# Block 0 of a fused SSM and GEGLU kernel: gate/up with the contraction outermost over three token tiles and 512 columns, in place of two tiles and 896 columns

## The chip, the cores and the metric

One core of one Trainium2 chip. The metric is the device time of one execution in microseconds; the kernel before is given by the median of five runs.

## The reference

```python
def reference(A_x, A_Lambda_re, ..., B_w_gate, B_w_up, B_w_down):
    def _A_ref(x, Lambda_re, Lambda_im, B_re, B_im, C_re, C_im, log_dt, Dskip):
        ...
        Bu = jnp.einsum("bld,pd->blp", x + 0j, B_bar)
        for t in range(L):
            h = Lam_bar[None, :] * h + Bu[:, t, :]
            hs.append(h)
        hseq = jnp.stack(hs, 1)
        return 2.0 * jnp.einsum("blp,dp->bld", hseq, Cmat).real + x * Dskip[None, None, :]

    def _B_ref(x, w_gate, w_up, w_down):
        return (_gelu(x @ w_gate) * (x @ w_up)) @ w_down

    x = A_x                        # 1 x 2048 x 512, bf16
    xn = _layernorm(x, axis=-1)
    return x + _A_ref(xn, ...) + _B_ref(xn, B_w_gate, B_w_up, B_w_down)
```

The token count is 2048, the width D is 512, the state size P is 512 and the hidden width F of the gated part is 1376. All inputs and the output are bf16.

## The kernel before

The 2048 tokens are four blocks of 512, and a block is four tiles of 128 tokens. For each block the kernel normalizes the rows (VectorE, with a power on GpSimd), transposes them to XNT by DMA, multiplies by the gate and up weights (`GU`), by the input matrix of the state recurrence (`BU`), scans the states on VectorE (`CHAIN`), and multiplies hidden values and states by the output matrices into one bank per tile (`DN`), which VectorE adds to the skip term and SP stores. PSUM has eight banks of 512 f32 columns.

An operation is declared with what it reads and writes. A list scheduler (`Sched`) orders VectorE, ScalarE and GpSimd by estimated durations and priorities; TensorE and SP issue in the order of the program text. `order_behind` and `ch` fix an order on one engine where the text wants one. SP's queue carries nearly all DMAs, ScalarE's queue the second X tile and three parameter rows.

Block 0 is handled apart, since nothing is there to overlap with at the start. Its gate/up product for the first 896 columns uses rows that are only centred: `cent` and `sub` subtract the mean, `cent_T` transposes a tile on TensorE into PSUM and an engine (ScalarE but for the first piece) copies it to XC, and the scale 1/sqrt(var) of a token is put in later, because a token is a PSUM partition here. `GT_k` is one matmul of one contraction slice k (128 of the 512), tile j and column range u of `FR` (three ranges of 256 columns, one of 128), for gate, up or both side by side; `GT_mm` is a whole unit, all four slices of one tile and range into one bank. `GT_evac` evicts a unit: a GELU with the scale on ScalarE (L718), a product with the scaled up half on VectorE (L724), into H0. Later `H0_T` transposes H0 by DMA.

The text order of block 0 before is this. Two tiles (0 and 1) have all seven 128-column pieces accumulated with k outermost, in seven banks (`acc`: three per tile, one shared for the 128-wide ranges): k = 0 gate then up, k = 1 gate then up, k = 2 and k = 3 both at once. `GT_evac` follows each range as k = 3 ends. Tiles 2 and 3 then run as units, each behind the eviction of the bank it takes. The weights come in slices of 896 columns per k (`ld_wk`, 224 KB each, gate and up in turn on SP), and one load each for columns 896 to 1376 (`ld_w`). The X tiles 2 and 3 are loaded ahead of and behind the last pair of slices.

The statistics of tiles 0 and 1 give a first `root` (L613, L614, L619), whose scales `rss` the evictions need; tiles 2 and 3 have their own. `norms` (L626) writes the normalized rows of a tile, and `TR` (L737) transposes them by DMA into XNT. The four of block 0 go through SP in turn, and `GU(0, [7, 8, 9, 10])` (L844), the columns from 896 on, follows block 0's units on TensorE and reads all of XNT of block 0. From there on TensorE's order is `GU`, `BU`, `DN` of the blocks, and this text is the same in both kernels.

Of the kernel before, what the change touches and what calls it, by code (L numbers as in the profile page):

```python
# [9 lines left out]
ALU = mybir.AluOpType  # L10
# [351 lines left out]
def build(nc, ins, out):  # L362
    with ExitStack() as es:
# [15 lines left out]
        WD = A.alloc("WD", [KF, D], BF16)  # L379
        FS = 896  # L380
        WGc = [Buf("WGc%d" % i, "sbx", 10 * i, 10 * i + 1) for i in range(KD + 1)]
        WUc = [Buf("WUc%d" % i, "sbx", 100 + 10 * i, 101 + 10 * i) for i in range(KD + 1)]
        wdeps = lambda Wc, ft: Wc[0:KD] if 128 * ft < FS else [Wc[KD]]
        WDc = [Buf("WDc%d" % i, "sbx", 200 + 10 * i, 201 + 10 * i) for i in range(2)]
# [96 lines left out]

        def ld_wk(W, Wc, src, k, queue="sync", after=()):
            return S.dma(lambda e: e.dma_start(W.ap[:, k, 0:FS], src[128 * k:128 * (k + 1), 0:FS]),
                         256 * FS, writes=[Wc[k]], tag="ld_w", queue=queue, after=after)

        def ld_w(W, Wc, src):
            return S.dma(lambda e: e.dma_start(W.ap[:, :, FS:F], src[:, FS:F].rearrange("(k p) f -> p k f", p=128)),
                         1024 * (F - FS), writes=[Wc[KD]], tag="ld_w")

        def ld_x0(j, queue="sync", after=()):  # L490
            return S.dma(lambda e, j=j: e.dma_start(X[j].ap, x2[128 * j:128 * (j + 1), :]), 128 * 1024, writes=[X[j]], tag="ld_x0", queue=queue, after=after)
        ld_x0(0)
        GATE["par"] = S.order_behind(ld_x0(1, "scalar", [wrm]), GATE["table"])
        for k in range(KD):
            if k == 3:
                ld_x0(2)
            ld_wk(WG, WGc, ins["B_w_gate"], k)
            ld_wk(WU, WUc, ins["B_w_up"], k)
        ld_x0(3)

# [20 lines left out]
        def load_W():  # L521
            ld_w(WG, WGc, ins["B_w_gate"])
            ld_w(WU, WUc, ins["B_w_up"])

# [164 lines left out]
        def acc(j, u):  # L689
            return (3, 256 * j) if u == 3 else (4 * j + u, 0)  # L690

        def GT_k(k, j, u, ws, first=False):
            f0, f1 = FR[u]
            w = f1 - f0
            bank, c0 = acc(j, u)
            dst = PS[bank][:, c0 + w * ws[0]:c0 + w * (ws[-1] + 1)].rearrange("p (w f) -> p w f", w=len(ws))
            PE(lambda e: e.matmul(dst, XCd(j, k), WGU[:, ws[0]:ws[-1] + 1, k, f0:f1], start=first, stop=k == KD - 1, skip_group_check=True),  # L697
               d_pe([w * len(ws)]), [(WGc, WUc)[w_][k] for w_ in ws] + [XCs[j][k > 0]] + ([] if first else [BANK[bank]]), [BANK[bank]], "GK")

        def GT_mm(j, u, bank):  # L700
            f0, f1 = FR[u]
            w = f1 - f0
            dst = PS[bank][:, 0:2 * w].rearrange("p (w f) -> p w f", w=2)

            def f(e):
                ins_ = None
                for k in range(KD):
                    ins_ = e.matmul(dst, XCd(j, k), WGU[:, :, k, f0:f1], start=(k == 0), stop=(k == KD - 1))  # L708
                return ins_
            PE(f, d_pe([2 * w] * KD), WGc[0:KD] + WUc[0:KD] + XCs[j], [BANK[bank]], "GT")  # L710

        def GT_evac(js, r, bank, rss, c0s=(0,)):
            f0, f1 = FR[r]
            w = f1 - f0
            todo, gelus = [], []
            for j, (sc, rb), c0 in zip(js, rss, c0s):
                GATE["nh"] = kk = (GATE["nh"] + 1) % 3
                gelus.append(ACT(lambda e, kk=kk, c0=c0, sc=sc: e.activation(GG[kk].ap[:, 0:w], PS[bank][:, c0:c0 + w], ACTF.Gelu_apprx_tanh, scale=sc),  # L718
                                 d_act(w, 1), [BANK[bank], rb], [GG[kk]], "gelu"))
                todo.append((j, sc, rb, c0, kk))  # L720
            GATE["last_gelu"] = gelus[-1]
            for j, sc, rb, c0, kk in todo:
                hp = Buf("H0_%d_%d" % (j, r), "sb", H0[j].lo + 2 * f0, H0[j].lo + 2 * f1)
                V(lambda e, j=j, kk=kk, c0=c0, sc=sc: e.scalar_tensor_tensor(H0[j].ap[:, f0:f1], PS[bank][:, c0 + w:c0 + 2 * w], sc, GG[kk].ap[:, 0:w],  # L724
                                                                             ALU.mult, ALU.mult),
                  d_dve_1x(w), [BANK[bank], GG[kk], rb], [hp], "hmul", after=gelus)

# [79 lines left out]
        def GU_rest(b):  # L807
            k2, ft = b % 2, KF - 1
            f0, m = 128 * ft, FROWS[ft]
            for i in range(2):  # L810
                bank = next_bank()

                def f(e, i=i, bank=bank):
# [6 lines left out]
                    return ins_  # L820
                PE(f, d_pe([2 * m] * 8), [WGc[KD], WUc[KD]] + XTr(b), [BANK[bank]], "GR%d" % b)
                GATE["nh"] = kk = (GATE["nh"] + 1) % 3
# [149 lines left out]
        fill(4)  # L972
        GT_k(0, 0, 0, [0], True)
        cent_T(1, 0, 1, 6)
        for u in (1, 2, 3):
            GT_k(0, 0, u, [0], True)
        cent_T(0, 1, 4, 7)
        cent_T(1, 1, 4, 5)
        for u in range(4):
            GT_k(0, 0, u, [1])  # L980
        for us in ((0, 3, 2), (1,)):
            for w_ in range(2):
                for u in us:
                    GT_k(0, 1, u, [w_], w_ == 0 and u < 3)
        ch(*stats(0, 0)); ch(*stats(0, 1))
        op, mn0, qb0, rq0 = root(0, 0, 2)
        ch(op)
        ch(recip(qb0, rq0))
        for j in range(2):
            ch(norms(0, [j], mn0, rq0, 0))  # L990
        TR(0, [0, 1])
        ch(*stats(0, 2)); ch(sub(2))
        ch(*stats(0, 3)); ch(sub(3))
        op, mn2, qb2, rq2 = root(0, 2, 4)
        ch(op)
        ch(recip(qb2, rq2))
        rss = [(rq.ap[:, i:i + 1], rq) for rq in (rq0, rq2) for i in range(2)]
        for w_ in range(2):
            for j in range(2):
                for u in range(4):  # L1000
                    GT_k(1, j, u, [w_])
        for j in range(2):
            for u in range(4):
                GT_k(2, j, u, [0, 1])
        for j, u in ((0, 0), (0, 1), (0, 2), (1, 0), (1, 1), (1, 2), (0, 3), (1, 3)):
            if (j, u) == (1, 0):
                cent_T(2, 0, 4, 7)
            GT_k(3, j, u, [0, 1])
            if u < 3:
                GT_evac([j], u, acc(j, u)[0], rss[j:j + 1])  # L1010
        GT_evac((0, 1), 3, 3, rss[0:2], (0, 256))
        def unit(j, u, bank):
            GT_mm(j, u, bank)
            GT_evac([j], u, bank, rss[j:j + 1])
        unit(2, 0, 0)
        unit(2, 1, 1)
        cent_T(3, 0, 4, 7, c0=512)
        for (j, u), bank in zip([(2, 2), (2, 3), (3, 0), (3, 1), (3, 2), (3, 3)], (2, 4, 5, 6, 3, 7)):
            unit(j, u, bank)
        rstate["n"] = 0  # L1020
        norms(0, [2, 3], mn2, rq2, 2)
        TR(0, [2, 3])
# [90 lines left out]
```

## Time and profile before

| What | Value |
|---|---|
| median of five runs | 178.16 us (177.79, 177.87, 178.16, 179.15, 179.3) |
| profiled execution's own time | 178.16 us |
| its span | 176.8 us, 2527 instructions |
| TensorE busy | 173.7 us, 98% |
| VectorE busy | 159.2 us, 90% |
| ScalarE busy | 95.2 us, 54% |
| first matmul of block 0's gate/up | 4.56 us |
| first L844 matmul | 18.94 us |

The span runs from the first to the last instruction of the program; the own time is longer by what lies around it. "PE" is TensorE, "PEld" its weight loads, "DVE" VectorE, "ACT" ScalarE, "POOL" GpSimd and "SP" the engine that issues DMAs. Matmuls overlap one another in the profile: each is drawn until its modelled end, so the distance between the starts of two matmuls, not the length of one, is what a matmul takes of TensorE's time. A line of the timeline or of the chain has the start, the length and the instruction, with the idle time before it and its releaser in brackets.

### The profile page before, as it was taken

The page shows a single profiled execution, that of the slowest core. Times are in us where ns is not written, and L with a number is a line of the kernel's source. Part 1 is how long each engine was busy: PE and PEld are TensorE (multiplying, and loading weights), DVE is VectorE, ACT ScalarE, POOL GpSimd, SP SyncE. Part 2 cuts the span into 40 slices and gives each one's busy share as a digit, 9 for nine tenths or more (in the row PEclk, how much of TensorE's full clock was granted, in tenths as well). Part 3 has the DMA queues.
Part 4 walks back from the last instruction along what each step waited for, and adds up shares of the span by engine and source line. Part 5 has one row for each costly group of instructions (what it writes and reads, how often), then busy time and mean ns, then how long its engine had stood idle before and what let it go on. Part 6 is the DMA issues. An engine that isn't in the chain of part 4 may idle for free.

```text
span 176.8 us, 2527 instructions
## 1 busy us (share of the span) xinstructions
PE 173.7 (98%) x895; PEld 85.3 (48%) x895; DVE 159.2 (90%) x279; ACT 95.2 (54%) x185; POOL 10.3 (6%) x24
## 2 busy tenths in 40 slices
PE   8999999999999999999999999999999999999995
PEld 3845464644644444444644444444464444444453
DVE  5779799995989999879999999989999999999931
ACT  4258576999976899257676594000657880000000
POOL 3222040200300000000200000000000000000000
PEclk9999999999999999999999999999999999999999
DMA  5994799178599500001134000002001000000311
GB/s 176 360 280 63 200 193 206 33 140 155 112 227 333 97 0 2 0 30 59 33 61 89 0 0 0 4 0 89 30 0 33 0 0 0 0 0 0 122 67 54
DMA packets 31364, 14.36 MB, mean 81 GB/s; under 512 B 23704, under 2 KB 31352, under 8 KB 31352
## 3 DMA queue, kind: packets, MB, share of 16 engines
q1 hardware_dynamic: 31184, 14.07, 33.4%
q8 instruction: 7, 0.11, 0.3%
q10 hardware_dynamic: 168, 0.13, 0.2%
q14 instruction: 5, 0.04, 0.1%
HBM read 6.46 MB, written 2.10 MB: 48 GB/s over the span
## 4 chain that ended last, share of the span: by engine, by line
PE 95%; DMA 2%; DVE 1%; ACT 1%; issue 0%; DVEq 0%
PE PS L885 37%; PE PS L844 32%; PE PS L750 16%; PE PS L697 3%; PE PS L818 3%; DMA arena<-arena 2%; PE PS L934 2%; DVE arena L724 1%; PE PS L676 1%; PE PS L708 1%; ACT arena L718 0%; PE PS L941 0%; ACT arena L683 0%; DVE arena L626 0%; DVE arena L903 0%
## 5 line engine op out<-in xcount | busy, mean ns | idle before, releaser
L885 PE MATMUL PS<-arena 128*128 128x512 bf16 (+3 forms) x323 | 66.2, 367 | 0.0
L844 PE MATMUL PS<-arena 128*128 128x512 bf16 x264 | 58.1, 380 | 0.3 <-DMA arena<-arena 0.3
L885 PEld LDWEIGHTS PS<-arena 128*128 128x128 bf16 (+1 forms) x323 | 30.8, 98 | 35.2
L844 PEld LDWEIGHTS PS<-arena 128*128 128x128 bf16 x264 | 25.7, 98 | 30.8 <-issue 0.5
L788 DVE TENSOR_TENSOR_SCAN arena<-arena 128x512 bf16<-128x512 f32 x32 | 38.7, 1254 | 0.0
L859 ACT ACTIVATE arena<-PS 128x512 bf16<-128x512 f32 x33 | 19.8, 600 | 25.6 <-DVE arena L903 16.1
L750 PE MATMUL PS<-arena 128*128 128x512 bf16 (+1 forms) x136 | 28.1, 367 | 0.0
L863 ACT ACTIVATE arena<-PS 128x512 bf16<-128x512 f32 x33 | 19.8, 600 | 5.5 <-PE PS L844 5.5
L750 PEld LDWEIGHTS PS<-arena 128*128 128x128 bf16 x136 | 13.3, 98 | 14.1
L877 ACT ACTIVATE PS<-arena 128x512 f32<-128x512 bf16 (+2 forms) x17 | 9.4, 575 | 18.6 <-DVE arena L903 18.1
L759 ACT ACTIVATE arena<-PS 128x512 bf16<-128x512 f32 x32 | 17.8, 592 | 2.0 <-PE PS L750 2.0
L903 DVE TENSOR_TENSOR arena<-PS,arena 128x512 bf16<-128x512 f32 (+2 forms) x17 | 10.9, 653 | 7.3 <-PE PS L885 7.2
L865 DVE TENSOR_TENSOR arena<-arena 128x512 bf16<-128x512 bf16 x33 | 13.2, 418 | 2.1 <-ACT arena L863 2.1
L777 DVE TENSOR_TENSOR arena<-arena 128x4096 bf16<-128x4096 bf16 (+1 forms) x5 | 9.2, 1861 | 0.9 <-ACT arena L603 0.9
L775 DVE TENSOR_TENSOR arena<-arena 128x4096 bf16<-128x4096 bf16 (+1 forms) x5 | 9.2, 1861 | 0.3 <-ACT arena L602 0.3
L800 DVE TENSOR_TENSOR arena<-arena 128x4096 bf16<-128x4096 bf16 x4 | 9.2, 2289 | 0.0
L801 DVE TENSOR_TENSOR arena<-arena 128x4096 bf16<-128x4096 bf16 x4 | 9.2, 2288 | 0.0
L607 DVE BATCH_NORM_STATS2 arena<-arena 128x6 f32<-128x512 bf16 x12 | 7.8, 680 | 1.1 <-DMA arena<-in_A_x_dram 0.9
L718 ACT ACTIVATE arena<-PS,arena 128x256 bf16<-128x256 f32 (+1 forms) x16 | 6.3, 446 | 4.4 <-DVE arena L608 3.7
L724 DVE SCALAR_TENSOR_TENSOR arena<-PS,arena 128x256 bf16<-128x256 f32 (+1 forms) x16 | 6.4, 445 | 1.0 <-PE PS L676 0.7
L697 PE MATMUL PS<-arena 128*128 128x256 bf16 (+2 forms) x48 | 7.2, 301 | 0.0
L708 PE MATMUL PS<-arena 128*128 128x512 bf16 (+1 forms) x32 | 6.5, 353 | 0.0
(96 smaller groups left out, 126.2 us busy)
## 6 DMA issues: line engine op xcount, KB each, us to landing
out_dram<-arena SPq DMA_DIRECT2D x15, 128.0 KB, 1.7
arena<-in_A_x_dram SPq DMA_DIRECT2D x3, 512.0 KB, 5.4
arena<-in_B_w_down_dram SPq DMA_DIRECT2D x1, 1280.0 KB, 7.9
arena<-in_B_w_gate_dram SPq DMA_DIRECT2D x4, 224.0 KB, 4.1
arena<-in_B_w_up_dram SPq DMA_DIRECT2D x4, 224.0 KB, 4.2
arena<-in_B_w_gate_dram SPq DMA_DIRECT2D x1, 480.0 KB, 5.7
arena<-in_B_w_up_dram SPq DMA_DIRECT2D x1, 480.0 KB, 6.5
arena<-arena SPq DMA_TRANSPOSE x25, 3.0
```

Source lines behind the costliest of these rows:

```text
L697: PE(lambda e: e.matmul(dst, XCd(j, k), WGU[:, ws[0]:ws[-1] + 1, k, f0:f1], start=first, stop=k == KD - 1, skip_group_check=True), d_pe([w ...
L750: ins_ = e.matmul(PS[bank][:, 128 * j0:128 * j1], BBT[c][dk].ap[:, 128 * s:128 * (s + 1)], XNT[b].ap[:, dk, 128 * j0:128 * j1], start=(dk ...
L759: GATE["evBu"] = ACT(lambda e, bank=bank, k3=k3, s=s, c=c: e.activation(SSc[k3][s][c].ap, PS[bank][:, :], ACTF.Copy), d_act(512), [BANK[ba ...
L775: V(lambda e, s0=s0, s1=s1: e.tensor_tensor(TA.ap[:, s0:s1], ssb.ap[:, s0:s1], cos4[:, s0:s1], ALU.mult), d_dve_tt2x(1024 * step), [ss, CO ...
L788: V(lambda e, g=g, rb=rb, init=init: e.tensor_tensor_scan(g.ap, rb, g.ap, init, ALU.mult, ALU.add), d_dve_scan(512), [g, PA[RRr]] + ([CARc ...
L844: ins_ = e.matmul(PS[bank][0:m, c0:c1], W.ap[:, dk, 128 * ft:128 * ft + m], XNT[b].ap[:, dk, c0:c1], start=(dk == 0), stop=(dk == KD - 1))
L859: GATE["last_gelu"] = ACT(lambda e, bg=bg, kk=kk, m=m: e.activation(GG[kk].ap[0:m, :], PS[bg][0:m, :], ACTF.Gelu_apprx_tanh), d_act(512), ...
L863: ACT(lambda e, bu=bu, kk=kk, m=m: e.activation(UPB[kk].ap[0:m, :], PS[bu][0:m, :], ACTF.Copy), d_act(512), [BANK[bu]], [UPB[kk]], "evU")
L865: V(lambda e, kk=kk, m=m, ft=ft, k2=k2: e.tensor_tensor(HTt[k2][ft].ap[0:m, :], GG[kk].ap[0:m, :], UPB[kk].ap[0:m, :], ALU.mult), d_dve_tt ...
L877: ACT(lambda e: e.activation(PS[bank][:, c0:c1], X[tt].ap[:, c0:c1], ACTF.Copy), d_act(c1 - c0), [X[tt]], [BANK[bank]], "seed")
L885: ins_ = e.matmul(PS[bank][:, c0:c1], l_[:, 128 * j:128 * (j + 1)], r_[:, c0:c1], start=False, stop=last and n == len(ops) - 1, skip_group ...
L903: V(lambda e: e.tensor_tensor(OUTB[ko].ap[:, c0:c1], PS[bank][:, c0:c1], XD[tt].ap[:, c0:c1], ALU.add), d_dve_1x(c1 - c0), [BANK[bank], XD ...
```

## The change

The contraction-outermost part takes three tiles (0, 1 and 2) and the first 512 columns, two banks for each tile, six in all. Slices of the weights are loaded per k for 512 columns (128 KB), columns 512 to 896 come as one load for gate and one for up, and columns 896 to 1376 as before. The X tile 2 is now loaded ahead of the second pair of slices, tile 3 ahead of the fourth. One `root` serves tiles 0 to 2, another tile 3. What is left, both halves of tile 3 and columns 512 to 896 of all tiles, runs as ten units. `GT_evac` takes one unit at a time. The diff, cut to its core:

```diff
-        FS = 896
-        ...
-        wdeps = lambda Wc, ft: Wc[0:KD] if 128 * ft < FS else [Wc[KD]]
+        FC = [(0, 512), (512, 896), (896, F)]
+        ...
+        wdeps = lambda Wc, ft: Wc[0:KD] if ft < 4 else [Wc[KD + (ft > 6)]]
...
         for k in range(KD):
-            if k == 3:
-                ld_x0(2)
+            if k in (1, 3):
+                ld_x0((k + 3) // 2)
             ld_wk(WG, WGc, ins["B_w_gate"], k)
             ld_wk(WU, WUc, ins["B_w_up"], k)
-        ld_x0(3)
+        ld_w(WG, WGc, ins["B_w_gate"], 1)
+        ld_w(WU, WUc, ins["B_w_up"], 1)
...
         def acc(j, u):
-            return (3, 256 * j) if u == 3 else (4 * j + u, 0)
+            return 2 * j + u
...
-        GT_k(0, 0, 0, [0], True)
+        def ks(k, j, w_, first=False):
+            for u in range(2):
+                GT_k(k, j, u, w_, first)
+        ks(0, 0, [0], True)
         cent_T(1, 0, 1, 6)
-        for u in (1, 2, 3):
-            GT_k(0, 0, u, [0], True)
+        ks(0, 0, [1])
         cent_T(0, 1, 4, 7)
+        ks(0, 1, [0], True)
         cent_T(1, 1, 4, 5)
-        for u in range(4):
-            GT_k(0, 0, u, [1])
-        for us in ((0, 3, 2), (1,)):
-            for w_ in range(2):
-                for u in us:
-                    GT_k(0, 1, u, [w_], w_ == 0 and u < 3)
-        ch(*stats(0, 0)); ch(*stats(0, 1))
-        op, mn0, qb0, rq0 = root(0, 0, 2)
+        ks(0, 1, [1])
+        for j in range(2):
+            ks(1, j, [0, 1])
+        ch(*stats(0, 2)); ch(sub(2)); ch(*stats(0, 0)); ch(*stats(0, 1))
+        op, mn0, qb0, rq0 = root(0, 0, 3)
         ch(op)
+        ch(*stats(0, 3)); ch(sub(3))
         ch(recip(qb0, rq0))
+        op, mn3, qb3, rq3 = root(0, 3, 4)
+        ch(op)
+        rss = [(rq0.ap[:, i:i + 1], rq0) for i in range(3)] + [(rq3.ap, rq3)]
         for j in range(2):
             ch(norms(0, [j], mn0, rq0, 0))
+        ch(recip(qb3, rq3))
         TR(0, [0, 1])
-        ch(*stats(0, 2)); ch(sub(2))
-        ...
-        for w_ in range(2):
-            for j in range(2):
-                for u in range(4):
-                    GT_k(1, j, u, [w_])
+        cent_T(2, 0, 4, 7)
         for j in range(2):
-            for u in range(4):
-                GT_k(2, j, u, [0, 1])
-        for j, u in ((0, 0), (0, 1), (0, 2), (1, 0), (1, 1), (1, 2), (0, 3), (1, 3)):
-            ...
-            GT_k(3, j, u, [0, 1])
-            if u < 3:
-                GT_evac([j], u, acc(j, u)[0], rss[j:j + 1])
-        GT_evac((0, 1), 3, 3, rss[0:2], (0, 256))
-        ...
-        unit(2, 0, 0)
-        unit(2, 1, 1)
-        cent_T(3, 0, 4, 7, c0=512)
-        for (j, u), bank in zip([(2, 2), (2, 3), (3, 0), (3, 1), (3, 2), (3, 3)], (2, 4, 5, 6, 3, 7)):
-            unit(j, u, bank)
-        rstate["n"] = 0
-        norms(0, [2, 3], mn2, rq2, 2)
+            ks(2, j, [0, 1])
+        for k in range(3):
+            ks(k, 2, [0, 1], k == 0)
+        for j in range(3):
+            ks(3, j, [0, 1])
+            for u in range(2):
+                GT_evac(j, u, acc(j, u))
+            if j == 0:
+                cent_T(3, 0, 4, 6)
+        for (j, u), bank in zip([(3, 0), (3, 1), (0, 2), (0, 3), (1, 2), (1, 3), (2, 2), (2, 3), (3, 2), (3, 3)],
+                                (7, 6, 0, 1, 2, 3, 4, 5, 0, 7)):
+            GT_mm(j, u, bank)
+            GT_evac(j, u, bank)
+        rstate["n"] = 2
+        norms(0, [2], mn0, rq0, 0)
+        norms(0, [3], mn3, rq3, 3)
         TR(0, [2, 3])
```

## The prediction, as it was put on record

> **What bounds the kernel now.** I read the busy shares first, then the chain that ended last in order of time, then the waits of TensorE, and last the timelines of the opening, matmul by matmul.
>
> ```profile
> PE 173.7 (98%) x895; PEld 85.3 (48%) x895; DVE 159.2 (90%) x279; ACT 95.2 (54%) x185; POOL 10.3 (6%) x24
> PEclk9999999999999999999999999999999999999999
> ```
>
> TensorE is busy for 98% of a span of 176.8 us. The profiled execution's own time is 178.16 us, which is also the median of the five runs; 1.36 us lie around the span. A busy TensorE is not one at its peak, so I looked for lost time in its start times.
>
> ```profile
> 18.80 0.14 issue
> 18.94 5.34 PE PS L844 x24
> ...
> 129.76 12.09 PE PS L844 x56
> 141.85 32.91 PE PS L885 x171
> 174.75 0.02 issue
> ```
>
> These are pieces of the chain: start, length, what. From 18.94 us to 174.75 us it is TensorE alone. Take 56 matmuls of 512 columns in 12.09 us: 0.216 us each. All pieces behind 18.94 run at this rate with no hole, so whatever the change does must show in when the first L844 (the remaining gate/up columns of block 0 from the transposed tile) starts, or as a new wait behind it.
>
> ```profile
> 0.77 3.14 PE L934 MATMUL PS<-const-bfloat16-1.0 128*128 128x512 bf16 x7 [0.77 <-PEq L1098]
> ...
> 4.56 0.37 PE L697 MATMUL PS<-arena 128*128 128x256 bf16 x1
> 6.01 0.32 PE L697 MATMUL PS<-arena 128*128 128x256 bf16 x1
> ...
> 12.69 0.38 PE L708 MATMUL PS<-arena 128*128 128x512 bf16 x1
> 13.07 0.38 PE L708 MATMUL PS<-arena 128*128 128x512 bf16 x1
> 18.27 0.38 PE L708 MATMUL PS<-arena 128*128 128x256 bf16 x2
> 18.94 0.59 PE L844 MATMUL PS<-arena 128*128 128x512 bf16 x2 [0.29 <-DMA arena<-arena]
> ```
>
> The timeline gives start, length and count. The seven warming matmuls start 0.427 us apart, twice 0.216, so TensorE runs at half rate at first although the granted clock reads full throughout; single starts show the full rate from about 6.1 us. After that there are three holes, by start to start less the matmul's own column time: 7.20 to 7.26 (0.07), 12.91 to 13.07 (0.17, waiting for a bank's eviction), and 18.48 to 18.94 (0.46). The column "idle" shows only 0.29 of the last, because the modelled end of a matmul lies behind its column time. Together 0.69 us: all that an order of work in block 0 can win back at an unchanged clock.
>
> ```profile
> PE PS L844 <- DMA arena<-arena: 0.3, 1, 0.3
> PEld PS L708 <- ACT arena L718: 0.5, 1, 0.5
> 13.62 0.16 DVE L619 RECIPROCAL arena<-arena 128x2 f32<-128x2 bf16 x1
> 14.93 0.40 DVE L626 TENSOR_SCALAR arena<-arena 128x512 bf16<-128x512 bf16 x1
> ```
>
> The last hole waits for the fourth transposing DMA of block 0. Its source, the normalized tile 3, is ready at 15.33 us, and that DMA lands 3.3 us after its issue at 15.49.
>
> **The change, part by part.**
>
> *Column work.* Both orders put 28,672 columns of gate/up and the same 16 transposes through TensorE. 80 matmuls become 68. One of 256 columns starts 0.109 after its forerunner, one of 512 0.216, so twelve fewer save 12 x 0.002 = 0.02 us. Up to 6.1 us both orders are at half rate with work at hand, so the end of block 0 moves only by holes.
>
> *Loads.* SP's thirteen loads ahead of the transposes become fifteen; two more issues at 0.47 us put the transposing queue entries back from 7.04 to 7.98. The first of these has its data from the norm, which I place at 10.3 us, so that is hidden; without this cover it costs 0.9. For landings I use bytes in queue order: before, 480 KB had landed at 4.0 us, 704 at 5.4, 928 at 6.2, 1152 at 6.7, 1376 at 7.2, 1600 at 7.9, 2304 at 9.8. After, first up slice: 512 KB, 4.2 to 4.6 us; X tile 2: 640 KB, 5.0; second pair: 896 KB, 6.1; third: 1152 KB, 6.7; X tile 3: 1280 KB, 7.0; fourth: 1536 KB, 7.7; columns 512 to 896: 2304 KB, 9.8.
>
> *TensorE's new order,* from the unchanged 4.56 us. The first up slice is wanted at 5.08 (two matmuls at 0.21, one transpose at 0.107): there. The first contraction of both tiles ends at 6.56. The second needs tile 0's evicted transposes: their last ends at 6.03, ScalarE takes 0.49, so TensorE goes on at 6.60: a wait of 0.04, where before sixteen matmuls covered this eviction. Tile 1's eviction ends at 6.98, wanted at 7.03. The second pair of weights is wanted at 6.60 (0.5 spare). Transposes of tile 2 at 7.46, third contraction 7.69 to 8.55 (weights 1.0 spare), tile 2's eviction (0.60) ends at 8.48. Tile 2's three contractions end at 9.85, the fourth wants its weights then (2.1 spare). Tile 3's transposes at 10.28, contractions to 11.37, its eviction ends at 11.25. Ten units remain: two of four 512-column matmuls (1.73) to 13.09, then four pairs of a 512 and a 256 unit (0.86 + 0.44) to 18.28.
>
> *VectorE.* Tile 2's statistics now come first: 5.0 + 0.69 + 0.18 + 0.35 is 6.3, wanted at 7.46. Two more statistics (0.87 each), root (0.17 + 0.71 on GpSimd, covered by tile 3's statistics and subtraction, 1.3) and reciprocal give the scales at 9.8; the first GELU wants them at 10.26. Sixteen products at about 0.41 run from 10.8, three normalizations between. Each bank is wanted a unit of 0.43 to 0.86 us later than its product ends: bank 0 at 13.09 against 11.2, bank 4 at 15.69 against 13.8. So the 0.17 hole goes. Tile 3 is normalized at about 13.4 in place of 15.33; its transposing DMA, at 3.3 to 4.1 us, lands at 16.8 to 17.6, before 18.28. So the 0.46 hole goes. One wait is new in VectorE's queue: a parameter product now stands ahead of six products and waits for GpSimd's power, which waits for the parameters' transpose (13.4 before, some 14 now, plus 1.0). It is reached at 15.7. Queued behind it are the products that free bank 2 for L844; these have 1.9 us spare.
>
> *Behind 18.28.* The next X load leaves SP some 2 us earlier, so VectorE's 0.95 us idle at 21.5 shrinks. ScalarE's sine table and VectorE's scans had their results early: 69.9 against a use at 74.4, and 162.0 against 165.4. A shift of 0.7 breaks none.
>
> The sum: 0.69 + 0.02 - 0.04 = 0.67, taken as 0.65 us. 178.16 - 0.65 = **177.5 us**.
>
> A rule of the Trainium skill speaks against the change ("DMA: Bandwidth & Descriptors", section "Bandwidth"): batch transfers to 1 MiB or more, 64 KB reaching 138 GB/s and 1 MB 341, measured there on loads that GpSimd issued. Were 128 KB loads limited to 138 GB/s, 1536 KB would land at about 13.4 us (an estimate, with 2 us fixed), 3.5 us late, and the sum would read 181. The trace has many loads in flight at once, so I do not take it:
>
> ```profile
> 4.56:6.10 1.54, 1.54 (x13) 1.41 (x13) 1.51 (x5) 0.28 (x1) 0.00 (x0) 1.00 0.97 336
> ```
>
> 336 GB/s with 224 KB loads queued; no row has 128 KB loads alone. From below, each can land no sooner than the first X tile, 2.1 us after issue: no wait either, the same sum. From above, each could keep the latency after issue that the 224 KB loads had (3.7 to 4.4 us); that is the first rival.
>
> **The rivals.**
>
> 1. *The loads are no quicker.* The second up slice lands at 3.08 + 4.1 = 7.2, not 6.6: 0.6 lost; the third at 4.02 + 4.4 = 8.4, another 0.1. The gain is used up: **178.2 us**. For it: SP's issue at 0.47 us each paces small loads. Against: the latencies rose with the bytes queued, and those are fewer.
>
> 2. *The wait before L844 stays.* If the last transposing DMA takes the 5.3 us that block 0's first took, it lands at 13.45 + 5.3 = 18.75, and 0.14 us is left of the gain: **178.0 us**. Against: that first one had loads ahead of it until 12.9.
>
> 3. *Slower: the clock.* Should the first up slice land at 1.66 + 3.7 = 5.4, TensorE stands still for 0.3 us at 5.08, longer than any hole it had before 6.1 (0.19, ahead of 4.56). If the full rate needs the 5.3 us of nearly unbroken work seen from 0.77 to 6.1 over again, half rate lasts to 10.7: 4.6 us at half rate cost 2.3. 178.16 - 0.65 + 0.3 + 2.3 = **180.1 us**. It decides from a landing later than about 5.3 us.
>
> On this the Trainium skill ("TensorE: Matmul & The Clock Gate", Part 1: The HAM clock gate) says that a free-running window of about 3.4 us decides, not a length of unbroken work since the start. By it one more window at half rate would cost 1.7 us, 179.5 in place of 180.1, and a run's luck would move the moment of full rate.
>
> That the change does nothing is excluded: the instruction lists show 68 matmuls and the split loads.
>
> **How the numbers follow.** A measurement of this kernel tells about 1% from no change. Forecast 0.56 (own range 177.1 to 177.9); rival 1 0.16, rival 2 0.08, rival 3 0.10; 0.10 for what I have not seen, half on each side. Within 1% (176.4 to 179.9) lie the forecast and rivals 1 and 2: 0.80. Slower 0.10 + 0.05 = 0.15, faster 0.05: a gain of 1.8 us has no place in the holes. The range's low end takes 0.75 us of the half rate between 4.56 and 6.1 away as well: 176.8. Its high end is rival 1 with the 1.1 us by which the runs of before exceeded their median: 179.3. Rival 3 and what is unseen stay outside, 0.2.
>
> **What would show it.** Right: the first L844 near 18.3 us with no DMA wait, tile 3 normalized near 13.4, no hole over 0.1 between 6.1 and 18.3, and everything behind shifted alike. Rival 1: TensorE idle for a DMA of weights at 6.6. Rival 3: 256-column matmuls still 0.21 apart behind 6.5 us. The prediction is wrong if block 0 ends at 18.3 and a hole opens later, at the sine tables (35 to 46 us) above all.

## The result, and the profile after

| What | before | after |
|---|---|---|
| median over all comparisons | 177.91 us (90 runs) | 177.41 us (48 runs) |
| ratio, 95% interval | | 0.9964, 0.9952 to 0.9975 |
| profiled execution's own time, span | 178.16, 176.8 us | 177.23, 175.9 us |
| first L844 (after: L842) | 18.94 us | 18.27 us |

The gain is 0.50 us by the medians, 0.36%. It is shown, and under the 1% that a measurement of a few runs tells from no change. The forecast was a gain of 0.65 us and 177.5 us. The long runs are gone as well: 12 of the 90 runs before took 179.0 us or more (up to 179.56; 4 of 75 in the runs of before that go with the experiments below), while the longest of the 48 after took 178.44. By the means the gain is 0.65 us (178.03 to 177.38).

The page of the kernel after, engines' busy time and counts, and from its last part the loads of weights (count, KB each, median us from issue to landing):

```profile
PE 173.2 (98%) x883; PEld 84.1 (48%) x883; DVE 159.7 (91%) x279; ACT 95.5 (54%) x185; POOL 10.7 (6%) x24
...
arena<-in_B_w_gate_dram SPq DMA_DIRECT2D x4, 128.0 KB, 2.9
arena<-in_B_w_up_dram SPq DMA_DIRECT2D x4, 128.0 KB, 3.2
```

There are twelve matmuls fewer. Before, the slices of 224 KB took 4.1 us (gate) and 4.2 us (up) by the median; the smaller ones land a microsecond sooner after their issue.

Pieces of the chain after (start, length, what):

```profile
6.31 0.22 PE PS L700 x2
6.53 0.05 issue
6.58 1.02 PE PS L700 x4
...
129.09 12.09 PE PS L842 x56
141.18 32.91 PE PS L883 x171
174.08 0.02 issue
```

The 56 matmuls of this L842 piece take the same 12.09 us as before and begin 0.67 us earlier (129.09 against 129.76), as L842 itself does: in this pair TensorE's work behind block 0 is unchanged. The span is 0.9 us shorter; the other 0.2 us lie behind the last matmul (2.06 us to the end of the span against 2.29), and a section below takes them up.

The waits after (engine, line, waited for: us in total, times, longest), and the timelines of TensorE and VectorE (start, length, what, idle time and its releaser in brackets):

```profile
DVE arena L553 <- POOL arena L552: 0.8, 1, 0.8
PE PS L932 <- PEq L1089: 0.8, 1, 0.8
PEld PS L700 <- ACT arena L686: 0.5, 2, 0.3
```

```profile
17.83 0.60 PE L711 MATMUL PS<-arena 128*128 128x256 bf16 x4
18.27 0.59 PE L842 MATMUL PS<-arena 128*128 128x512 bf16 x2
```

```profile
9.31 0.17 DVE L622 RECIPROCAL arena<-arena 128x3 f32<-128x3 bf16 x1
...
12.92 0.40 DVE L629 TENSOR_SCALAR arena<-arena 128x512 bf16<-128x512 bf16 x1
...
16.32 0.16 DVE L553 TENSOR_TENSOR arena<-arena 128x4 f32<-128x4 bf16 x1 [0.78 <-POOL arena L552]
```

L842 starts with no wait for a DMA; before, L844 had one. Tile 3 is normalized at 13.32 us (15.33 before), and its transposing DMA lands at 16.69 us, 1.6 us ahead of its use. One hole is left from 6.1 us on: 0.22 us at 6.58, where the second contraction of tile 0 waits for ScalarE's eviction (L686). VectorE's new wait for GpSimd is there, 0.78 us, and TensorE has no hole behind it ahead of L842.

### The profile page after: what moved, and what is told of

It is laid out like the page before. It is cut to its first block, busy times and chain, and to the rows that moved or that the text cites. A ratio compares the mean times of both kernels' runs of the same rounds, so it can differ in the third digit from the quotient of the medians.

```text
span 175.9 us, 2509 instructions
## 1 busy us (share of the span) xinstructions
PE 173.2 (98%) x883; PEld 84.1 (48%) x883; DVE 159.7 (91%) x279; ACT 95.5 (54%) x185; POOL 10.7 (6%) x24
## 4 chain that ended last, share of the span: by engine, by line
PE 98%; DVE 0%; issue 0%
PE PS L883 37%; PE PS L842 32%; PE PS L748 16%; PE PS L711 4%; PE PS L700 3%; PE PS L816 3%; PE PS L932 2%; PE PS L679 1%; PE PS L939 0%; DVE arena L901 0%
## 5 line engine op out<-in xcount | busy, mean ns | idle before, releaser
L842 PE MATMUL PS<-arena 128*128 128x512 bf16 x264 | 58.1, 380 | 0.0
L842 PEld LDWEIGHTS PS<-arena 128*128 128x128 bf16 x264 | 25.7, 98 | 30.3
L748 PE MATMUL PS<-arena 128*128 128x512 bf16 (+1 forms) x136 | 28.1, 367 | 0.0
L711 PE MATMUL PS<-arena 128*128 128x512 bf16 (+1 forms) x40 | 7.1, 337 | 0.0
L700 PE MATMUL PS<-arena 128*128 128x512 bf16 (+1 forms) x28 | 6.6, 366 | 0.1
```

What stands on the lines that cost most here:

```text
L748: ins_ = e.matmul(PS[bank][:, 128 * j0:128 * j1], BBT[c][dk].ap[:, 128 * s:128 * (s + 1)], XNT[b].ap[:, dk, 128 * j0:128 * j1], start=(dk ...
L842: ins_ = e.matmul(PS[bank][0:m, c0:c1], W.ap[:, dk, 128 * ft:128 * ft + m], XNT[b].ap[:, dk, c0:c1], start=(dk == 0), stop=(dk == KD - 1))
```

## Three executions of each kernel: what belongs to the program

One profiled execution is one draw. Each kernel was profiled twice more, and one further kernel (`e8_sp_shift`, below) has block 0 exactly as before. "Full rate from" is the start of the first matmul of block 0, transposes included, from which starts lie 0.056 us (128 columns), 0.109 us (256) or 0.216 us (512) apart; holes are those behind it. In some profiles the records of 15 matmuls are missing (TensorE x880 in place of x895); each leaves a gap of 0.216 us that is no hole, and where it was the first L844 or L842, its start is put that much ahead of the first one shown.

| execution | full rate from | holes ahead of L844 / L842 | L844 / L842 | 4th transposing DMA landed | last matmul's start to end of span | own time |
|---|---|---|---|---|---|---|
| before | 6.16 | 0.07 + 0.17 + 0.46 | 18.94 | 18.80 | 2.29 | 178.16 |
| before_again | 4.62 | 0.28 + 0.17 | 18.05 | 17.56 | 2.35 | 177.43 |
| before_third | 4.67 | 0.05 + 0.17 | 17.88 | 17.38 | 2.50 | 177.53 |
| e8_sp_shift | 5.36 | 0.07 + 0.17 | 18.19 | 17.68 | 2.12 | 177.20 |
| after | 5.58 | 0.22 | 18.27 | 16.69 | 2.06 | 177.23 |
| after_again | 4.77 | 0.15 + 0.07 | 17.88 | 16.94 | 2.06 | 176.84 |
| after_third | 5.37 | 0.11 + 0.11 + 0.21 | 18.38 | 16.96 | 2.05 | 177.50 |

For after, L842 starts at 17.56 us + half of (full rate from, less 4.6) + holes in all three executions, to 0.02 us (the expectation had put 17.75 in place of 17.56); for before the constant comes out between 17.47 and 17.62. The constants agree, so the column work of block 0 is the same in both kernels. Behind block 0 there are three more holes: 0.08 us at 32.4 in before_again, 0.17 at 24.5 in before_third, 0.14 at 32.8 in after_third.

What was expected of the further executions:

> The kernel before once more, for a second profile of the same program. Theory (the moment of TensorE's full rate moves from execution to execution, 4.6 to 6.2 us in the profiles so far, and costs half of its distance; the rest is holes): with an earlier full rate the holes of before are not smaller than 0.69 us in sum, since the weights and the normalizations do not come earlier with it. Rival: the holes are the same three with the same lengths whatever the clock does.

> The kernel after, unchanged, looked at a second time: which of its readings belong to the program and which to one execution. Theory (the end of block 0 is set by TensorE's column work plus its holes, and the moment of full rate is free): the first L842 starts at 17.75 + half of (moment of full rate - 4.6) + holes, so between 17.8 and 18.8 us for a moment between 4.6 and 6.6; no wait for a transposing DMA ahead of it (landed by 17.3 at the latest); one hole of 0.1 to 0.3 at tile 0's eviction near 6.6 when full rate comes before 6.0, none above 0.1 when it comes later. Rival (full rate comes earlier because of the new order of work): full rate again within 0.2 us of the 5.58 us of the first look.

> The kernel before, unchanged, looked at a third time. Theory (two limits that change places with the moment of full rate): with full rate before 5.2 us a hole of 0.2 to 0.4 at the first up slice and the last transposing DMA of block 0 landed in 2.4 to 2.6 us; with full rate after 6 us no hole there. The wait ahead of L844 goes by the landing of that DMA alone: 3.3 us or more and it is there with 0.3 to 0.5 us, 2.6 us or less and it is gone. Rival (the wait belongs to the program): L844 again waits 0.3 to 0.5 us for the DMA, whatever the moment.

> The kernel after, unchanged, looked at a third time, for the same question as its second look: first L842 between 17.8 and 18.8 us, at 17.75 + half of (moment of full rate - 4.6) + holes; no wait for a transposing DMA. Rival: the moment of full rate again within 0.2 us of 5.58 us.

Two of these were missed: the holes of before_again add up to 0.45 us ahead of L844, not to 0.69 or more, and before_third, with early full rate, had 0.05 us at the first up slice in place of 0.2 to 0.4 (its part on the transposing DMA, 2.5 us and no wait, was met). The two of after were met in the range of L842's start, in the absence of a wait for a transposing DMA, and against their rival (full rate at 4.77 and 5.37 us, not within 0.2 us of 5.58); the constant, and in after_again the holes, came out otherwise.

The 0.46 us wait ahead of L844 is not a constant of the kernel before. This is line L737, its transposing DMAs issued between 13 and 17 us, in the first execution of before, then in the second:

```profile
L737 SPq DMA_TRANSPOSE arena<-arena x2: 1189/1680/2172, 14.3 to 15.5; - x2
...
DMA to landing us min/median/max: 3.3/3.7/4.1
```

```profile
L737 SPq DMA_TRANSPOSE arena<-arena x2: 1191/1228/1264, 13.8 to 15.1; - x2
...
DMA to landing us min/median/max: 2.4/2.5/2.5
```

The same two DMAs need 3.3 and 4.1 us in one execution, 2.4 and 2.5 in the other, and in the second L844 waits for none. The DMA view shows what sets the slow ones apart; the first execution of before, 14 to 19 us (a queue with packets, MB and share; DMAs with median us to landing):

```profile
q8 instruction: 1, 0.02, 1.3%
...
arena<-arena SPq DMA_TRANSPOSE x2, 3.7
```

The first line is one packet of 16 KB on a queue (q8) of kind "instruction", at 16.20 us, while packets of the third transposing DMA were still being moved. Such a packet falls among the packets of a transposing DMA of tile 2 or 3 in three of this study's 14 profiles, and these are the three with a slow one: before (16.20 us, 4.1 us to landing), e1 (14.87, 4.3) and e6 (19.56, 4.0), the latter two described below. In the other eleven it comes when the data of these DMAs has been moved, at 17.11 us at the earliest (e3), and none of them has a delay of this kind. The fourth DMA of before, issued behind the third, landed 0.47 us after it. No run moved this packet alone, so its part is seen in all profiles but not tested; what places it was not found.

The second execution has a hole of its own instead; the waits and TensorE's timeline of before_again:

```profile
PEld PS L697 <- DMA arena<-in_B_w_up_dram: 0.3, 1, 0.3
```

```profile
5.05 0.50 PE L676 MATMUL PS<-arena 128*128 128x128 bf16 x6
5.67 0.28 PE L697 MATMUL PS<-arena 128*128 128x256 bf16 x1
```

Full rate came early, TensorE ran out of work at 5.39 us, and the first up slice landed at 5.62. In before_third it landed at 5.44 and the hole was 0.05: the landing decides there, and not the moment of full rate alone, as the expectation had put it. So the kernel before has two loose ends, the first up slice and tile 3's transposing DMA, each late in some executions. In after the up slice landed at 4.39 to 4.76 us and the DMA 0.9 to 1.6 us ahead of L842 in all three. That margin is what the change has for certain; what it is worth differs from execution to execution. It fits the long runs that only before has, but none of those was profiled, so what made them long is not shown.

## Experiments on block 0

The ratios below are each against runs of before on the same chip, with their 95% interval.

**Is the early normalization enough?** e1 puts the root of tiles 2 and 3, and their normalization, ahead of products in the kernel before, with its loads as they are. e2 only lets the transposes of tile 3 fill the 0.17 us hole. e3 does both. (In e1, e3 and e6 two parameter products on VectorE are also held until the last GELU, so that they don't take the place that is made free.)

```diff
# e1_norm_early, on before; root (and norm of tile 2) as a condition of an early product
+        early[0, 0] = op
...
+                early[1, 0] = norms(0, [2], mn2, rq2, 2)
...
+        norms(0, [3], mn2, rq2, 2)
...
-        norms(0, [2, 3], mn2, rq2, 2)
```

```diff
# e2_fill, on before
         unit(2, 0, 0)
-        unit(2, 1, 1)
         cent_T(3, 0, 4, 7, c0=512)
+        unit(2, 1, 1)
```

> The kernel before, with its loads and its order on TensorE, but with tiles 2 and 3 normalized earlier on VectorE (root ahead of the first product, tile 2's normalization ahead of the fourth). Theory (the gain of the change is holes on TensorE, the largest the wait of the first L844 for the fourth transposing DMA): that DMA is issued near 14.9 us in place of 15.49 and lands near 18.3, the hole of 0.46 us shrinks to below 0.1, the hole of 0.17 at 12.9 stays; about 177.5 us against 177.9 (ratio 0.998). Rival (the gain comes from the smaller, earlier weight loads): no change, ratio 1.000.

> The kernel before with one swap on TensorE: the four transposes of tile 3 stand between the two first units of tile 2, where the hole of 0.17 us is. Theory: that hole closes, but the first L844 still waits for the fourth transposing DMA, which is set by tile 3's normalization and SP's queue and not by TensorE; the 0.17 us go to that wait, ratio 1.000 (177.9 us), L844 at the same 18.9 us with a hole of 0.6. Rival (each hole counts by itself): 0.17 us faster, ratio 0.999.

> Both edits in the kernel before. Theory: both holes close, the first L844 starts near 18.3 to 18.4 us, and the time is that of the changed kernel, 177.3 to 177.5 us, ratio 0.9965, with two tiles, 896 columns and 224 KB loads left as they were. Rival (loads or contraction order bring the gain): no faster than 177.7.

Measured: e1 177.46 us, ratio 0.9972 (0.9952 to 0.9991); e2 177.79, 0.9994 (0.9967 to 1.002); e3 177.71, 0.9992 (0.9976 to 1.0009).

e1 came as expected (0.998): it is faster than before by its interval, and no run tells its gain from that of the whole change (0.9964, 0.9952 to 0.9975). In its profile the third transposing DMA is a slow one again (4.3 us), yet the fourth lands at 17.71, and L846 (before's L844) starts at 18.01 us without a wait for it: normalized earlier, the tile has margin. Two other waits are there:

```profile
PE PS L752 <- DMA arena<-arena: 0.8, 1, 0.8
PE PS L708 <- DVE arena L726: 0.2, 1, 0.2
```

The second, 0.36 us by starts, is the edit's own price (a product held back by the root, and so a bank). The first, 0.93 us by starts, is in block 1, at 33.22 us. These are block 1's transposing DMAs in e1, then in before (duration of the issue: min, median, max in ns; first and last start):

```profile
L739 SPq DMA_TRANSPOSE arena<-arena x4: 1197/1268/2981, 25.0 to 30.6; - x4
```

```profile
L737 SPq DMA_TRANSPOSE arena<-arena x4: 1197/1266/1399, 25.8 to 29.8; - x4
```

VectorE had normalized all four tiles by 26.4 us, and e1's first issue is earlier than before's; but its second one took 2.98 us in place of 1.40, and so the last DMA landed at 33.09 (32.28 in before). Why that issue was long is not shown.

e2 closes its hole, but its profile has others, 0.07, 0.18 and 0.11 us, and the DMAs at 2.4 and 2.5 us, so there was no wait to see: its ratio, with 1.000 and 0.999 both inside the interval, does not tell the theory from its rival. e3 was a miss: 177.3 to 177.5 was expected. Its profile has a first unit of tile 2 that starts 0.53 us late, since the product that frees its bank waits for the root, and that for X tile 3 (landed 10.36 us), and two holes of 0.28 and 0.25 for weights that landed late. In that execution the early root on the old load order cost what it brought. e1 and e3, whose intervals overlap, leave open what early normalization is worth with the old loads.

**Are the smaller loads needed?** e4 is after with slices of 896 columns again; all else, the order of X and of TensorE included, is after's. e7 is before with after's order of statistics, roots and X loads.

```diff
# e4_loads896, on after
-        FC = [(0, 512), (512, 896), (896, F)]
+        FC = [(0, 896), (896, F)]
...
-        ld_w(WG, WGc, ins["B_w_gate"], 1)
-        ld_w(WU, WUc, ins["B_w_up"], 1)
```

```diff
# e7_stats_order, on before (roots and norms as in after)
-            if k == 3:
-                ld_x0(2)
+            if k in (1, 3):
+                ld_x0((k + 3) // 2)
...
-        ch(*stats(0, 0)); ch(*stats(0, 1))
-        op, mn0, qb0, rq0 = root(0, 0, 2)
+        ch(*stats(0, 2)); ch(sub(2)); ch(*stats(0, 0)); ch(*stats(0, 1))
+        op, mn0, qb0, rq0 = root(0, 0, 3)
```

> The changed kernel with the weight slices of 896 columns (224 KB) again; X tiles 2 and 3 and TensorE's order stay as in the change. By bytes in queue order the first up slice lands at 5.4 us, wanted at 5.1 to 5.2; X tile 2 at 5.8; the second up slice at 7.0, the third at 8.2, wanted at 6.6 and 7.7. Theory (loads only have to be in time): TensorE stands still for about 0.3 us at 5.1 and 0.1 to 0.2 twice later, L844 starts 0.5 us later than in the change, about 177.9 us, ratio to before 1.000. Rival 3 of the prediction (a hole of 0.3 us before full rate starts the 5.3 us over): half rate until some 10.7 us, 2 us more, about 179.9 us. If the loads do not matter at all: 177.4 us.

> The kernel before with one part of the change alone: the order of the statistics, roots and normalizations and the places of X tiles 2 and 3 in SP's queue are the change's; contraction order, tiles, columns on TensorE and 224 KB slices are those of before. Theory (the wait for the last transposing DMA is most of the gain, and it comes from the statistics): tile 3 is normalized near 14.4 us, when its transposes have been read, L844 starts near 18.5 in place of 18.94; about 177.5 us, ratio 0.9975. Rival (the smaller slices bring the gain: weights are late in many executions of before): X tile 2 now stands ahead of the second pair of slices and makes this no better, 177.9 us or more.

Measured: e4 178.51 us, ratio 1.0031 (1.0012 to 1.0051); e7 178.21, 1.0024 (1.0000 to 1.0047). TensorE's timeline of e4, then of e7:

```profile
6.13 0.38 PE L698 MATMUL PS<-arena 128*128 128x256 bf16 x2
7.27 1.02 PE L698 MATMUL PS<-arena 128*128 128x512 bf16 x4 [0.76 <-DMA arena<-in_B_w_up_dram]
```

```profile
9.22 1.13 PE L696 MATMUL PS<-arena 128*128 128x512 bf16 x5 [0.37 <-DMA arena<-in_B_w_up_dram]
```

e4's second up slice landed at 7.18 us, and TensorE stood 0.92 us by starts: with 896-column slices the new order wants the second contraction before its weights are there. Holes of 0.4 to 0.7 us in all had been expected, and 177.9 us; this one alone was larger, and the forecast was missed. In e7 the fourth transposing DMA landed at 17.78, ahead of the last unit's end, as its theory said, but the gain that was expected with it (0.9975) did not come; the rival was right. X tile 2 now stands ahead of the second pair of weights, and the third up slice landed at 9.08 us (7.64 to 8.14 in the four executions of the table with block 0 as before), with 0.54 lost. These two parts of the change, each alone, are slower than before, by interval (e7's just touches 1) and by line; with both, the kernel gains. Early normalization without the move of the X tiles (e1) is not among them.

**Does tile 3's path to L842 decide when its margin is used up?** e6 is after with tile 3's normalization behind five more products (nine in place of four); e5 is after with tile 0's remaining transposes ahead of a matmul pair, to close the 0.22 hole.

```diff
# e6_norm_late, on after
-        norms(0, [3], mn3, rq3, 3)
+        S.order_behind(norms(0, [3], mn3, rq3, 3), prod[1, 2])
```

```diff
# e5_trans_early, on after
-        ks(0, 0, [1])
         cent_T(0, 1, 4, 7)
+        ks(0, 0, [1])
```

> The changed kernel with tile 3's normalization put behind the product of tile 1's third range on VectorE, about 16.9 us in place of 12.9 (two small parameter products are held back too, so that they don't stand in the way). Theory (the lane normalization, transposing DMA, L844 sets the end of block 0 once its slack of 1.6 us is used up): the DMA is issued near 17.3 us and lands near 19.8, L844 starts there in place of 18.3, about 179.0 us (1.6 us over the change; ratio to before 1.006). Rival (L844 is not held by that lane): 177.4 to 177.7 us.

> The changed kernel with one swap on TensorE: tile 0's three remaining transposes stand ahead of the first two up matmuls, not behind them, so that ScalarE evicts them 0.2 to 0.4 us earlier. Theory: the one hole that the change opened (0.22 us at 6.58 in its profile, waiting for that eviction) closes, and as nothing else is late (loads 0.5 us ahead, last transposing DMA 1.6 us ahead of L844), the time falls by 0.1 to 0.2 us, to about 177.25 us (ratio to before 0.9955). Rival (the hole belongs to the weights' landing, 6.17 us for the second up slice): the hole moves to the load and the time stays at 177.4.

Measured: e6 180.45 us, ratio 1.0147 (1.0121 to 1.0173); e5 177.23, 0.9976 (0.9962 to 0.999). In e6 the lines L735 and L842 of after are L737 and L844. VectorE's timeline of e6, the view of its line L737 from 17 to 19 us, and TensorE's timeline:

```profile
17.27 0.40 DVE L629 TENSOR_SCALAR arena<-arena 128x512 bf16<-128x512 bf16 x1
```

```profile
L737 SPq DMA_TRANSPOSE arena<-arena x1: 1189/1189/1189, 17.7 to 17.7; - x1
...
DMA to landing us min/median/max: 4.0/4.0/4.0
```

```profile
18.21 1.46 PE L711 MATMUL PS<-arena 128*128 128x512 bf16 x8 [0.71 <-DVE arena L725]
22.04 0.81 PE L844 MATMUL PS<-arena 128*128 128x512 bf16 x3 [2.37 <-DVE arena L558]
```

Normalized at 17.67, issued at 17.70, landed at 21.68. The line names L558 as the releaser, but this is one of the profiles with a matmul record missing: the true first L844 starts at 22.04 - 0.216 = 21.82, ahead of the end of L558 (21.95) and 0.14 behind the landing, the same distance as before's 18.80 to 18.94. The hole is 2.3 us. So the path does decide once its margin is gone. The size was missed (179.0 expected): the DMA took 4.0 us, not 2.5, with a 16 KB instruction packet among its own, and a late product cost 0.87 us more at 18.21. In e5's profile the hole at tile 0's eviction is gone, and one of 0.10 us stands at 7.06, ahead of tile 1's second contraction. But e6, which has after's order there, shows 0.10 us ahead of the same matmul, and full rate came late in both (6.03 and 6.6 us); so the profile does not tell what the swap did. e5's gain over before (0.5 us) is that of after, and a gain over after is not shown.

## Experiment on the end of the program

Over the executions above, L844 or L842 lies at 18.27 us on average in the four with block 0 as before and at 18.18 in those of after: a difference of 0.1, not 0.67. Another 0.26 us lies behind the last matmul (2.31 against 2.06). The DMA view from 172 to 178 us shows what differs; first before_third (GB/s in 40 slices of 0.15 us, queues with packets and MB, stores with KB and us to landing), then after_again:

```profile
GB/s 0 0 0 0 0 0 0 0 0 0 0 0 0 55 0 61 287 261 26 15 5 0 150 69 0 0 0 0 0 0 0 55 0 0 0 0 0 0 0 0
...
q14 instruction: 2, 0.02, 1.2%
...
out_dram<-arena SPq DMA_DIRECT2D x1, 96.0 KB, 2.1
out_dram<-arena SPq DMA_DIRECT2D x1, 32.0 KB, 1.7
```

```profile
GB/s 0 0 0 0 0 0 0 0 0 0 0 0 0 0 102 323 226 5 0 147 72 0 0 0 0 0 55 0 0 0 0 0 0 0 0 0 0 0 0 0
...
q14 instruction: 1, 0.01, 0.5%
...
out_dram<-arena SPq DMA_DIRECT2D x1, 96.0 KB, 1.6
out_dram<-arena SPq DMA_DIRECT2D x1, 32.0 KB, 1.4
```

The lone 55 in slice 14 is a packet of 8 KB on the queue of kind "instruction", at 174.03 us, between the issues of the last two stores (173.52 and 174.22). The first store lands 2.1 us after its issue instead of 1.6, and the issue of the second takes 0.60 us instead of 0.33. In after such a packet comes at 171 us, before these stores, and the next behind them. Of the 14 profiles of this study, the six with the packet between the two issues (before three times, e2, e4, e8) have 2.12 to 2.50 us from the last matmul's start to the end, the other eight 2.05 to 2.07. e8 tests whether the place of the packet goes by the number of SP's instructions, which after has two more of:

```diff
# e8_sp_shift, on before: one load in three, SP alone is changed
-            S.dma(lambda e: e.dma_start(WD.ap[0:96, 10, :], ins["B_w_down"][1280:F, :]), 96 * 1024, ...)
+            for a in (0, 32, 64): S.dma(lambda e, a=a: e.dma_start(WD.ap[a:a + 32, 10, :], ...), 32 * 1024, ...)
```

> The kernel before with one small load, far from block 0, split in three: SP issues two DMAs more, as the kernel after does, and nothing else is changed on any engine. Theory of the tail (the time from the last matmul's start to the end of the span is longer in before, 2.29, 2.35 and 2.50 us in three looks against 2.06, 2.06 and 2.05 in after, because a transfer of 8 KB of instructions falls between the last two stores; where it falls goes by the number of instructions on SP): the transfer moves to about 171 us, the last store is issued in 0.33 us, the last matmul's start to the end takes 2.05 to 2.1 us, and the ratio to before is 0.997 to 0.999 (0.2 to 0.45 us less), with block 0 as it was. Rival (the tail is a matter of the order of work in block 0, or of chance): the transfer stays between the two stores or the tail stays at 2.3 to 2.5 us, and the ratio is 1.000. If the tail shrinks, the part of the gain of after that belongs to block 0 is what is left of its 0.50 us.

Measured: 177.95 us, ratio 1.0002 (0.9974 to 1.0031). The DMA view of e8, same window:

```profile
q14 instruction: 2, 0.02, 0.7%
...
out_dram<-arena SPq DMA_DIRECT2D x1, 96.0 KB, 1.9
out_dram<-arena SPq DMA_DIRECT2D x1, 32.0 KB, 1.5
```

The packet stayed, at 174.17 us, between the issues at 173.65 and 174.35. So its place does not go by SP's count alone, and that step of the theory falls. What moves it in after was not found. That it goes with a longer end is seen in all 14 profiles, but its cost varies from 0.06 to 0.44 us over the 2.06, and no run shows what it is worth in the median.

## Why the prediction was right, point by point

- *The number.* 177.5 us was forecast and 177.41 measured. That they lie so near is in part luck: the sum starts from 178.16, the median of five runs, and that of 90 is 177.91; its gain of 0.65 us is 0.15 too large by the medians; the two errors go against each other. Part of the gain is also not where the sum had it (last point).
- *Where a gain can show.* Borne out for the pair of executions it was made on: L842 at 18.27 (18.28 predicted), and TensorE's work behind it shifted alike, 0.67 us by the chain. Not foreseen were the other 0.2 us of the span, behind the last matmul.
- *The holes, 0.69 us.* Right for the profiled execution of before, too large for the kernel. Of the two large terms, 0.46 for the transposing DMA was one draw: 0 in the two other executions and in e8. This is the term that was mis-sized. The 0.17 for the bank's eviction was there in all four and is gone in all three of after.
- *The start, "unchanged" at 4.56 us.* It was one draw too: block 0's first gate/up matmul came at 4.62 to 4.70 us in the other six executions of the table.
- *The new wait, 0.04.* It measured 0.22, 0.07 and 0.11 us. The instant was right (6.58 against 6.60); TensorE was there sooner, because full rate came at 5.58 and not at 6.1. With still earlier full rate a second hole stands ahead of it, 0.15 us at 5.47 and 0.11 at 5.75, which the prediction did not have. So one of its signs of being right, no hole over 0.1 us between 6.1 and 18.3, was not met: 0.22 in after, 0.11 and 0.21 in after_third.
- *Loads by bytes in queue order.* First up slice 4.76 (4.2 to 4.6 predicted), X tile 2 5.06 (5.0), second pair 6.17 (6.1), third 7.24 (6.7), X tile 3 7.60 (7.0), fourth 9.20 (7.7), columns 512 to 896 11.69 (9.8). Within 0.2 us for the first three, then 0.5 to 1.9 us optimistic. The spare of 2.1 us that was given to the fourth pair covered it in two executions; in after_third the fourth up slice landed at 9.80 and cost 0.21 us, where none was foreseen.
- *VectorE.* Scales at 9.48 (9.8), tile 3 normalized at 13.32 (13.4), the GpSimd wait where it was said, without effect. The next X load left SP at 15.50 (17.71 before).
- *Rival 1* (loads no quicker) did not come: 2.9 and 3.2 us from issue to landing. e4, with the old slices in the new order, comes nearest to it: its second up slice landed at 7.18 us (7.2 in the rival), and it took 178.51 us, against the 178.2 worked out for the rival.
- *Rival 2* (the wait stays) did not come; e6 shows its mechanism, at a price of 3.2 us between e6's and after's distances to their own runs of before.
- *Rival 3* (the clock starts over) did not come, but its condition did not arise either: the first up slice landed at 4.39 to 4.76 us in after, and no run here has a hole of 0.3 us within block 0's gate/up ahead of full rate. What is seen is holes behind it: the one of 0.28 us at 5.67 in before_again and e4's of 0.92 us at 7.27 were both followed by starts 0.109 or 0.216 us apart. The moment of full rate itself moved between 4.62 and 6.16 us in three executions of one kernel. The Trainium skill ("TensorE: Matmul & The Clock Gate", Part 1: The HAM clock gate) says of its window that it is free-running and the warm-up differs from run to run, by 500 ns to either side; these executions agree that it differs, and by more than that, 1.5 us from the first to the last.
- *The rule on transfer sizes* (the Trainium skill, "DMA: Bandwidth & Descriptors", section Bandwidth) gave 181 us. It was rightly not taken: with many in flight at once, the 128 KB loads landed 2.9 and 3.2 us after issue, the 224 KB ones 4.1 and 4.2, and e4, with the larger ones, was slower than before (1.0031).
- *What the prediction lacked.* It counted on block 0 alone. The own times of the table's seven executions differ by 0.39 us on average (177.58 in the four with block 0 as before, 177.19 in the three of after). About 0.12 us of it are holes (0.46 against 0.34, those further on included) and 0.26 us lie behind the last matmul; the rest is within the scatter. Seven executions with a spread of 0.7 to 1 us don't settle these shares. That the median gained is shown; how it divides, and so how much of it the named holes brought, stays open.

## What to carry to other kernels

Where the start of a kernel decides, contraction-outermost over more tiles lets the loads be cut smaller, and the order of statistics follows it; here the new order without the smaller loads, and the statistics with the X tiles moved up but the old loads, were each slower than before. Try the smallest part first all the same: normalizing two tiles earlier on VectorE (e1) gained about as much as the whole change, though e3, which contains it, did not. Price a hole from more than one execution: a wait for a DMA that is there in one profile can be absent in the next, and a change that gives every late arrival a margin gains only in the executions in which something was late. Look also behind the last matmul before giving all of a small gain to the place that was edited.

## What was not expected of the hardware

- A transposing DMA of 128 rows in SBUF needs 2.4 us from issue to landing in some executions, 4.0 to 4.3 in others, and the one queued behind it 3.3, for the same program at nearly the same time. In all three profiles with a slow one (before, e1, e6) a 16 KB packet of an "instruction" queue falls among its packets, and in none of the other eleven.
- The moment of full rate on TensorE: 4.6 to 6.6 us over 14 profiles whose warming matmuls are the same. Each microsecond of it costs half of one: a 256-column matmul takes 0.213 us ahead of it and 0.109 behind.
- An 8 KB packet on an "instruction" queue beside the last two stores goes with 0.06 to 0.44 us more at the end of the program.
- X tiles and weights share SP's queue in time: with one 128 KB tile moved ahead of it, the third up slice landed at 9.08 us (e7), against 7.64 to 8.14 in the four executions of the table with block 0 as before.
